# Top-k attention with a gated feed-forward block: the order of the left-over query tiles, the first loads, and where the weights' low words are converted

## The chip, the core and the metric

The kernel runs on one core of one Trainium2 chip. The metric is the time of one execution on the device, in microseconds (us). A core has a matrix engine (TensorE, PE in the profile), a vector engine (VectorE, DVE), an engine for pointwise functions (ScalarE, ACT), a general one (GpSimd, POOL) and one that here only issues transfers (SyncE, SP). Each works through its own list of instructions in order and waits where an operand or a buffer is not there yet. Matrix products land in PSUM, everything else is kept in SBUF, inputs and outputs lie in HBM and are moved by 16 DMA engines.

## The reference

Attention over 8 batches, 8 heads, 576 queries and keys of 64 elements, where each query keeps its 32 largest scores; then a feed-forward block over 4608 tokens.

```python
scores = scale * np.matmul(q, k.transpose(0, 1, 3, 2))            # (8, 8, 576, 576)
kth = np.partition(scores, -32, axis=-1)[..., -32:-31]
scores = np.where(scores >= kth, scores, -1e9)
attn = np.exp(scores - scores.max(-1, keepdims=True))
attn = attn / (attn.sum(-1, keepdims=True) + 1e-9)
x = np.matmul(attn, v)             # heads side by side: (4608, 512)
h = x @ w_in                       # w_in (512, 2048), given in 64-bit floats
g = h * np.clip(h + 3.0, 0.0, 6.0) / 6.0
out = g @ w_out                    # w_out (2048, 512), given in 64-bit floats
```

## The kernel before

**Tiles.** Two heads make a pair, two pairs a half of a batch. The 576 queries of a head are four tiles of 128 and a left-over of 64. A duo is one query tile of one half: four heads at 128 queries each, in two units of two rows of 576 scores. A left-over duo packs the 64 left-over queries of two heads into 128 partitions, so it has one row per unit instead of two, and half the work on VectorE. There are 80 duos: 64 full ones and 16 left-over ones.

**One duo.** `Duo.scores` (L201) multiplies on TensorE into the one five-bank PSUM tile `big` and copies to SBUF on ScalarE (L239, L242; L227, L228 for a left-over duo). `Duo.top` (L249) finds the 32 largest on VectorE: four rounds of MAX8 (L256), with MATCH_REPLACE8 (L260) between them. Then, late by a fixed number of slots: `shift` on GpSimd (L269, L272), `exp` on ScalarE (L279, L284), `inverse` on VectorE (L293), `weights` on GpSimd (L303, and a split into 16-bit halves, L312), `flip` as a DMA transpose (L318), `join` (L324, on ScalarE for the first unit, on GpSimd for the second), `values` on TensorE (L344) and `place` on ScalarE (L354).

**Slots.** The order of every engine's list is written out by a loop over duos and eight slots each (L576). Slot i of a duo issues one round of `top`; then come the delayed parts of earlier duos; in slot 1 the scores of the next duo. The delays are the tables at L538 to L551, in slots from the duo's start. For example, `weights` of the two units stand at 10 and 14, `join` at 15 and 19, `values` at 22 or 25; the last two duos have a shorter table.

**Feed-forward.** When both halves of a query tile have their values, a block of 128 tokens is queued (L480, L486): `feed_forward` (L358) cuts it into 16 pieces, eight of 8 products h (L371), eight of 2 products acc (L391). After every second h piece a gate follows on GpSimd (L385, L386), two pieces late. The loop issues pieces by a running sum (L609): one a slot while anything is queued, a little more when 24 or 48 pieces are queued, half of that in the slots of a left-over duo. What is left after the last slot is issued at the end (L612). Left-over tiles of an even batch and the odd one behind it share one block, in the tile `xr`.

**Weights.** They arrive as 64-bit floats and are turned into 32-bit ones in 32 chunks of 128 x 512 by `convert` (L96): a load into `st`, the high words' magnitude on ScalarE (L108) and clamped on GpSimd (L109), the low words on ScalarE (L111), two bit operations on VectorE (L117, L118), and an addition on GpSimd (L123). `convert_step` (L499) moves the stages on, once a slot from the first duo on. The temporaries `a` and `y` come from the pool `g` of eight buffers, which the feed-forward's `g` tiles use as well.

**The start.** L521 to L533: load the first pair (six transfers on SP's queue, k then q), start two weight chunks, load the second pair, transpose the first pair on TensorE into `big` and copy it out, three conversion steps and the scores of the first duo's two units among them.

**The order of duos** is the list built at L410 to L420, which the diff shows.

Of the kernel before, what the change touches and what calls it, by code (L numbers as in the profile page):

```python
# [8 lines left out]
AF = mybir.ActivationFunctionType  # L9
ALU = mybir.AluOpType  # L10
F32 = mybir.dt.float32
# [18 lines left out]
def kernel(  # L30
# [9 lines left out]
    nc = tc.nc  # L40
# [47 lines left out]
    def big():  # L88

        return ps_big.tile([P, 5 * 512], F32, tag="big", name="big")  # L90
# [5 lines left out]
    def convert(dst, src):  # L96

        st = kqpool.tile([P, 2 * WC], U32, tag="kq", name="st")
        nc.sync.dma_start(st[:], src)
        yield
        words = st[:].rearrange("p (n two) -> p n two", two=2)
        lo, hi = words[:, :, 0], words[:, :, 1]
        a = gpool.tile([P, WC], F32, tag="g", name="a")
        y = gpool.tile([P, WC], F32, tag="g", name="y")
        nc.scalar.activation(a[:], hi.bitcast(F32), AF.Abs)  # L108
        nc.gpsimd.tensor_scalar(a[:], a[:], HI_MOST, HI_LEAST, ALU.min, ALU.max)  # L109

        nc.scalar.activation(y[:], lo, AF.Copy, bias=2.0, scale=2.0**-51)  # L111
        yield

        au, yu = a[:].bitcast(U32), y[:].bitcast(U32)
        nc.vector.tensor_scalar(au, au, 3, None, ALU.logical_shift_left)  # L117
        nc.vector.scalar_tensor_tensor(  # L118
            out=yu, in0=hi, scalar=0x80000000, in1=yu,
            op0=ALU.bitwise_and, op1=ALU.bitwise_or,  # L120
        )
        yield
        nc.gpsimd.tensor_tensor(  # L123
            dst.bitcast(I32), a[:].bitcast(I32), y[:].bitcast(I32), ALU.add
        )

    def weight_chunks():
# [11 lines left out]
    class Pair:  # L139
# [3 lines left out]
            self.b, self.hp = b, hp  # L143
            self.vm, self.vr, self.kr = vms[hp], vrs[hp], krs[b % 2 * NHP + hp]

        def load(self):
            h0 = 2 * self.hp
            t = self.landed = kqpool.tile([P, 2 * J + 1, 2, D], F32, tag="kq", name="landed")
            for i, src in enumerate((k, q)):
                for hh in range(2):  # L150
                    nc.sync.dma_start(  # L151
                        t[:, i * J : (i + 1) * J, hh, :],
                        src[self.b, h0 + hh, 0:JP, :].rearrange("(p j) d -> p j d", j=J),
                    )
                nc.sync.dma_start(
                    t[i * R : (i + 1) * R, 2 * J, :, :],
                    src[self.b, h0 : h0 + 2, JP:S, :].rearrange("h s d -> s h d"),
                )
# [9 lines left out]
                    self.vr[hh * R : (hh + 1) * R, hh, :], v[self.b, h0 + hh, JP:S, :]  # L168
                )

        def transpose(self):
            kq = kqpool.tile([P, JP + S], F32, tag="kq", name="kq")
            self.kT, self.qT = kq[:, 0:JP], kq[:, JP : JP + S]
            ps = big()
            for j in range(2 * J + 1):
                rows = self.landed[:, j, :, :].rearrange("p h d -> p (h d)")
                nc.tensor.transpose(ps[:, j * P : (j + 1) * P], rows, ident[:])
            c0 = 2 * JP
            nc.scalar.copy(kq[:, 0:c0], ps[:, 0:c0])
            nc.scalar.copy(kq[:, c0 : c0 + R], ps[:, c0 + R : c0 + 2 * R])  # L180
            for hh in range(2):
                d = slice(hh * D, (hh + 1) * D)
                nc.scalar.copy(self.kr[d, hh, :], ps[d, c0 : c0 + R])

    class Duo:

# [14 lines left out]
        def scores(self, us=(0, 1)):  # L201

            if us[0] == 0:
                self.sc = scpool.tile([P, 2, 2 * (S + R)], F32, tag="sc", name="sc")
                self.den = mpool.tile([P, 2, 2], F32, tag="den", name="den")
            sc, nu = self.sc[:, us[0] : us[-1] + 1, :], len(us)
            ps = big()
            heads = [slice(0, D), slice(D, P)]
            qs = slice(self.qt * P, min(self.qt * P + P, S))
            banks = ps[:, 0 : 4 * 512].rearrange("p (n s) -> p n s", s=512)  # L210
            left = ps[:, 4 * 512 :]
            if self.rest:


                quarters = [
                    (i, hh, d, heads[u ^ hh])
                    for i, u in enumerate(us)
                    for hh, d in enumerate(heads)
                ]
                for i, hh, d, to in quarters:  # L220
                    pr = self.pairs[us[i]]
                    nc.tensor.matmul(banks[to, i, :], pr.qT[d, qs], pr.kT[d, :])
                for i, hh, d, to in quarters:
                    pr = self.pairs[us[i]]
                    nc.tensor.matmul(banks[to, 2 + i, 0:R], pr.qT[d, qs], pr.kr[d, hh, :])
                nc.gpsimd.memset(sc[:, :, S : S + R], 0.0)
                nc.scalar.copy(sc[:, :, 0:JP], banks[:, 0:nu, :])  # L227
                nc.scalar.copy(sc[:, :, JP:S], banks[:, 2 : 2 + nu, 0:R])  # L228
                return
            for i, u in enumerate(us):  # L230
                pr = self.pairs[u]
                nc.tensor.matmul(
                    left[:, i * P : (i + 1) * P], pr.qT[:, qs], pr.kr[:].rearrange("p h r -> p (h r)")
                )
            for i, u in enumerate(us):
                pr = self.pairs[u]
                for hh, d in enumerate(heads):
                    nc.tensor.matmul(banks[:, 2 * i + hh, :], pr.qT[d, qs], pr.kT[d, :])  # L238
            nc.scalar.copy(  # L239
                sc.rearrange("p u (h s) -> p (u h) s", h=2)[:, :, 0:JP], banks[:, 0 : 2 * nu, :]  # L240
            )
            nc.scalar.copy(  # L242
                sc[:, :, JP : JP + P], left[:, 0 : nu * P].rearrange("p (u r) -> p u r", r=P)
            )

        def row(self, u, t):
            return self.sc[:, u, t * S : (t + 1) * S]
# [162 lines left out]
    duos = []  # L410
    for b in range(B):
        halves = [pairs[b][0:2], pairs[b][2:4]]
        for qt in range(J):
            duos += [Duo(h, qt) for h in halves]


            if qt == (0 if b == B - 1 else J - 1) and not 2 < b < B - 1:
                duos += [Duo(h, J) for h in halves]
            elif 2 < b < B - 1 and qt % 2 == 0:
                duos.append(Duo(halves[qt // 2], J))  # L420
    assert J == NHP == 4
    per_batch = 2 * J + 2
    ND = len(duos)
# [68 lines left out]
    def land(count=1):  # L492

        for _ in range(min(count, len(chunks))):
            c = convert(*chunks.pop(0))
            next(c)
            landing.append(c)
# [21 lines left out]
        return pairs[b + 1][at - first] if b + 1 < B and 0 <= at - first < NHP else None  # L519

    first = pairs[0]  # L521
    first[0].load()
    land(2)
    first[1].load()
    first[0].transpose()
    convert_step()
    duos[0].scores((0,))
    convert_step()
    first[2].load()
    convert_step()  # L530
    first[1].transpose()
    duos[0].scores((1,))
    land()  # L533

# [41 lines left out]
    for m in range(ND + 3):  # L576
        u = duos[m] if m < ND else None
        for i in range(8):
# [2 lines left out]
            if m < 4:  # L581
                parts(8 * m + i, False)
            convert_step()
            if m == 0 and i == 0:
                first[3].load()
            if m == 0 and i in (1, 2):
                first[i + 1].transpose()
            if i == (4 if m == 0 else 1) and m + 1 < ND:
# [59 lines left out]
```

## Time and profile before

| What | us |
|---|---|
| Median of 9 runs | 1577.71 |
| Lowest, highest | 1576.16, 1578.34 |
| The profiled execution's own time | 1577.94 |
| Its span, first to last instruction | 1576.2 |
| VectorE busy | 1466.6 (93%) |
| TensorE busy | 1441.9 (91%) |
| GpSimd busy | 1144.9 (73%) |
| ScalarE busy | 1097.6 (70%) |

The profile is of one execution. "Busy" is the union of an engine's instructions; matmuls overlap one another and their ends are modelled, so a busy TensorE is not one at its peak. A line of the timeline gives the start in us, the duration, engine, source line, operation, output <- inputs, shapes and count, and in brackets the idle time before it with what ended it. A line of waits gives who waited for whom, with the total in us, the number of times and the longest. The mean granted TensorE clock was 0.962 of full speed.

### The profile page before, as it was taken

The page shows a single profiled execution, that of the slowest core. Times are in us where ns is not written, and L with a number is a line of the kernel's source. Part 1 is how long each engine was busy: PE and PEld are TensorE (multiplying, and loading weights), DVE is VectorE, ACT ScalarE, POOL GpSimd, SP SyncE. Part 2 cuts the span into 40 slices and gives each one's busy share as a digit, 9 for nine tenths or more (in the row PEclk, how much of TensorE's full clock was granted, in tenths as well). Part 3 has the DMA queues.
Part 4 walks back from the last instruction along what each step waited for, and adds up shares of the span by engine and source line. Part 5 has one row for each costly group of instructions (what it writes and reads, how often), then busy time and mean ns, then how long its engine had stood idle before and what let it go on. Part 6 is the DMA issues. An engine that isn't in the chain of part 4 may idle for free.

```text
span 1576.2 us, 28787 instructions
## 1 busy us (share of the span) xinstructions
PE 1441.9 (91%) x10272; PEld 1031.5 (65%) x10272; DVE 1466.6 (93%) x3105; ACT 1097.6 (70%) x1865; POOL 1144.9 (73%) x1264
## 2 busy tenths in 40 slices
PE   5355799879999999998999999998999999999899
PEld 3142666567767767676777777776777777776675
DVE  6999999999999999999999999999999999999700
ACT  6675776777877777777776786777776786777521
POOL 4868687777867777867687777867687777867841
PEclk9577899989999999999999999999999999999999
DMA  8652544444444543546254544445254444533410
GB/s 237 158 182 42 116 83 82 90 94 98 73 95 86 101 84 78 99 87 117 55 104 81 98 88 83 94 91 113 58 104 81 98 88 82 103 58 68 83 22 14
DMA packets 450319, 144.49 MB, mean 92 GB/s; under 512 B 433280, under 2 KB 441472, under 8 KB 450176
## 3 DMA queue, kind: packets, MB, share of 16 engines
q1 hardware_dynamic: 450176, 142.65, 43.8%
q8 instruction: 81, 1.33, 0.4%
q14 instruction: 62, 0.51, 0.1%
HBM read 45.09 MB, written 9.44 MB: 35 GB/s over the span
## 4 chain that ended last, share of the span: by engine, by line
DVE 78%; PE 12%; issue 4%; POOL 3%; ACT 2%; SPq 1%; DMA 0%; POOLq 0%
DVE m L256 40%; DVE wk L260 35%; PE acc L391 5%; PE h L371 5%; DVE y L118 1%; PE pv L344 1%; DVE a L117 1%; POOL e L312 1%; DVE den L293 1%; PE big L238 1%; POOL sc L303 1%; POOL eT L324 1%; ACT sc L284 1%; SPq L151 1%; POOL g L386 0%
## 5 line engine op out<-in xcount | busy, mean ns | idle before, releaser
L256 DVE MAX8 m<-wk 128x8 f32<-128x576 f32 x864 | 613.4, 747 | 2.2
L391 PE MATMUL acc<-w_out,g 128*128 128x512 f32 x1152 | 518.1, 601 | 18.1 <-POOL g L386 18.1
L371 PE MATMUL h<-xT,w_in 128*128 128x128 f32 x4096 | 482.8, 278 | 18.3 <-ACT xT L354 18.3
L371 PEld LDWEIGHTS h<-xT,w_in 128*128 128x128 f32 x4096 | 472.4, 194 | 40.6 <-ACT xT L354 18.3
L260 DVE MATCH_REPLACE8 wk<-m,wk 128x576 f32<-128x576 f32 x576 | 423.9, 743 | 0.0
L303 POOL TENSOR_SCALAR sc<-sc,den 128x576 f32<-128x576 f32 x288 | 214.0, 753 | 240.0 <-DVE den L293 221.3
L391 PEld LDWEIGHTS acc<-w_out,g 128*128 128x128 f32 x1152 | 213.5, 191 | 265.5 <-issue 238.4
L312 POOL COPY e<-sc 128x2304 uint16<-128x2304 uint16 (+1 forms) x192 | 320.4, 1679 | 10.2
L279 ACT ACTIVATE sc<-sc,m 128x576 f32<-128x576 f32 x288 | 209.9, 775 | 75.8 <-DVE m L256 75.4
L284 ACT ACTIVATE sc<-sc,shift 128x576 f32<-128x576 f32 x288 | 220.3, 768 | 52.4 <-POOL shift L272 50.5
L324 ACT COPY eT<-t 128x2304 uint16<-128x2304 uint16 (+1 forms) x82 | 216.0, 2634 | 44.1 <-DMA t<-e 39.5
L344 PE MATMUL pv<-eT,vm 128*64 128x128 f32 (+1 forms) x2560 | 164.0, 273 | 58.8 <-ACT eT L324 44.0
L260 DVE MATCH_REPLACE8 wk<-m,sc 128x576 f32<-128x576 f32 x288 | 211.9, 742 | 0.0
L344 PEld LDWEIGHTS pv<-eT,vm 128*64 128x64 f32 x2560 | 135.0, 141 | 110.4 <-ACT eT L324 48.2
L324 POOL COPY eT<-t 128x2304 uint16<-128x2304 uint16 (+1 forms) x78 | 203.9, 2614 | 4.2 <-DMA t<-e 4.0
L256 DVE MAX8 m<-sc 128x8 f32<-128x576 f32 x288 | 203.4, 743 | 1.7 <-ACT sc L242 1.7
L386 POOL TENSOR_TENSOR g<-g,hs 128x512 f32<-128x512 f32 x144 | 185.0, 1285 | 12.0
L379 ACT ACTIVATE g<-h,three 128x512 f32<-128x512 f32 x144 | 98.6, 684 | 134.3 <-PE h L371 123.6
L238 PE MATMUL big<-kq 64*128 64x512 f32 x512 | 136.1, 651 | 0.0
L239 ACT COPY sc<-big 128x2048 f32<-128x2048 f32 (+1 forms) x65 | 119.2, 1834 | 17.5 <-PE big L238 17.4
L385 POOL TENSOR_SCALAR g<-g 128x512 f32<-128x512 f32 x144 | 89.2, 620 | 51.8 <-ACT g L379 40.6
L381 ACT COPY hs<-h 128x512 f32<-128x512 f32 x144 | 83.6, 581 | 0.0
(47 smaller groups left out, 1026.2 us busy)
## 6 DMA issues: line engine op xcount, KB each, us to landing
landed<-in_k_dram SPq DMA_DIRECT2D x64, 128.0 KB, 3.1
landed<-in_q_dram SPq DMA_DIRECT2D x64, 128.0 KB, 3.0
st<-in_moe_w_in_dram SPq DMA_DIRECT2D x16, 512.0 KB, 5.1
vm<-in_v_dram SPq DMA_DIRECT2D x64, 128.0 KB, 2.4
st<-in_moe_w_out_dram SPq DMA_DIRECT2D x16, 512.0 KB, 6.2
out_dram<-o SPq DMA_DIRECT2D x32, 256.0 KB, 2.4
t<-e SPq DMA_TRANSPOSE x160, 4.6
landed<-in_k_dram SPq DMA_DIRECT2D x32, 32.0 KB, 2.9
```

The costliest lines, as they stand in the source:

```text
L238: nc.tensor.matmul(banks[:, 2 * i + hh, :], pr.qT[d, qs], pr.kT[d, :])
L256: nc.vector.max(self.m[u][:, t, 8 * r : 8 * r + 8], self.cur[t])
L260: nc.vector.match_replace(wk, self.m[u][:, t, 8 * r : 8 * r + 8], self.cur[t], LOWEST)
L279: nc.scalar.activation(row, row, AF.Prelu, bias=m[:, t, TOP_K - 1 : TOP_K], scale=-1.0, alpha=FLAT)
L284: nc.scalar.activation(row, row, AF.Exp, bias=self.less[u][:, t : t + 1], scale=-scale / FLAT, accum_out=self.den[:, u, t : t + 1],)
L303: nc.gpsimd.tensor_scalar(row, row, self.den[:, u, t : t + 1], 1.0, ALU.mult, ALU.mult)
L312: nc.gpsimd.tensor_copy(halves[:, :, to : to + c1 - c0], words)
L324: copy(eT[:, 0 : self.nb, :] .rearrange("p c q -> p (c q)") .bitcast(U16) .rearrange("p (x h) -> p h x", h=2), self.t16[u][:, 0 : 2 * self ...
L344: nc.tensor.matmul(pv[hh * D : (hh + 1) * D, u * w : (u + 1) * w], pr.vm[:, hh, c, :] if c < J else pr.vr[:, hh, :], rhs, start=(c == 0), ...
L371: nc.tensor.matmul(h[:, (f - f0) * P : (f - f0 + 1) * P], w_in[:, i, f * P : (f + 1) * P], xT[:, i, :], start=(i == 0), stop=(i == NHP - 1),)
L386: nc.gpsimd.tensor_tensor(g[:], g[:], hs[:], ALU.mult)
L391: nc.tensor.matmul(acc[:], gs[f // nf][:, f % nf * P : (f % nf + 1) * P], w_out[:, f, :], start=(f == 0), stop=(f == NFC - 1),)
```

## The change

Four things are changed.

1. The order of duos. Before, the left-over duos stood last in batches 0 to 2, one behind the first and one behind the third query tile in batches 3 to 6, and behind the first query tile in batch 7. Now they stand last in every even batch and first in every odd one, so that four of them follow one another at four places.
2. The start. VectorE zeroes a piece of `w_out`, and TensorE multiplies it twice into `big`, a result that nobody reads. The first pair's q is issued from ScalarE's queue, k from SP's. The loads of the second, third and fourth pair stand ahead of weight chunks that they stood behind. The first transposes go to three separate PSUM tiles, and what the first scores need is copied first; the remaining copies come behind the scores.
3. The first scores are copied out in three copies, the left-over keys first and then one head at a time.
4. In `convert`, the low words are converted into the destination (`dst`) instead of a temporary `y`, and the later steps work there in place.

```diff
@@ convert
-        y = gpool.tile([P, WC], F32, tag="g", name="y")
...
-        nc.scalar.activation(y[:], lo, AF.Copy, bias=2.0, scale=2.0**-51)
+        nc.scalar.activation(dst, lo, AF.Copy, bias=2.0, scale=2.0**-51)
...
-            out=yu, in0=hi, scalar=0x80000000, in1=yu,
+            out=dst.bitcast(U32), in0=hi, scalar=0x80000000, in1=dst.bitcast(U32),
...
-            dst.bitcast(I32), a[:].bitcast(I32), y[:].bitcast(I32), ALU.add
+            dst.bitcast(I32), a[:].bitcast(I32), dst.bitcast(I32), ALU.add
@@ Pair.load
-        def load(self):
+        def load(self, queue=None):
...
-            for i, src in enumerate((k, q)):
+            for i, (src, eng) in enumerate(((k, nc.sync), (q, queue or nc.sync))):
...
-                    nc.sync.dma_start(
+                    eng.dma_start(
@@ Pair.transpose
+            def turn(ps, tiles):
+                for i, j in enumerate(tiles):
+                    rows = self.landed[:, j, :, :].rearrange("p h d -> p (h d)")
+                    nc.tensor.transpose(ps[:, i * P : (i + 1) * P], rows, ident[:])
...
+            if first:
+                ps = [ps_w.tile([P, 512], F32, tag="w", name="kqp") for _ in range(3)]
+                turn(ps[0], range(J))
+                turn(ps[1], [J, 2 * J])
+                turn(ps[2], range(J + 1, 2 * J))
+                nc.scalar.copy(self.kT, ps[0][:])
+                nc.scalar.copy(kq[:, JP : JP + P], ps[1][:, 0:P])
+                copy_left(ps[1][:, P:])
+                self.later = [
+                    (kq[:, JP + P : c0], ps[2][:, 0 : JP - P]),
+                    (kq[:, c0 : c0 + R], ps[1][:, P + R : 2 * P]),
+                ]
+                return
@@ Duo.scores
+            if us == (0,):
+                (to, src), rest = copies
+                copies = [rest, (to[:, 0, :], src[:, 0, :]), (to[:, 1, :], src[:, 1, :])]
+            for copy in copies:
+                nc.scalar.copy(*copy)
@@ the order of duos
-        for qt in range(J):
+        for qt in [J, *range(J)] if b % 2 else range(J + 1):
             duos += [Duo(h, qt) for h in halves]
-            if qt == (0 if b == B - 1 else J - 1) and not 2 < b < B - 1:
-                duos += [Duo(h, J) for h in halves]
-            elif 2 < b < B - 1 and qt % 2 == 0:
-                duos.append(Duo(halves[qt // 2], J))
@@ the start
     first = pairs[0]
-    first[0].load()
-    land(2)
+    nc.vector.memset(w_out[:, 0, :], 0.0)
+    ps = big()
+    for _ in range(2):
+        nc.tensor.matmul(ps[:, 0:DM], w_out[:, 0, 0:P], w_out[:, 0, :])
+    first[0].load(nc.scalar)
     first[1].load()
-    first[0].transpose()
+    land()
+    first[2].load()
+    land()
+    first[0].transpose(first=True)
+    duos[0].scores((0,))
+    for copy in first[0].later:
+        nc.scalar.copy(*copy)
     convert_step()
-    duos[0].scores((0,))
+    first[3].load()
+    first[1].transpose()
     convert_step()
-    first[2].load()
-    convert_step()
-    first[1].transpose()
     duos[0].scores((1,))
     land()
@@ the loop over duos and slots
-            if m == 0 and i == 0:
-                first[3].load()
```

## The prediction

> **What bounds the kernel now.** I read the busy digits first, then VectorE's waits, then the two ends of the timeline. The page's second part, busy tenths in 40 slices of 39.4 us:
>
> ```profile
> PE   5355799879999999998999999998999999999899
> DVE  6999999999999999999999999999999999999700
> ```
>
> VectorE (DVE) is full from the second slice to the thirty-eighth, then stops while TensorE (PE) goes on. So there are three stretches: a head until DVE starts, a DVE stretch, a PE tail. What DVE waited for over the whole span (us in total, times, longest):
>
> ```profile
> DVE a L117 <- POOL a L109: 13.5, 2, 10.2
> DVE den L293 <- ACT den L289: 7.0, 2, 6.7
> DVE m L256 <- ACT sc L242: 1.7, 1, 1.7
> ```
>
> 10.2 us of the first row is the head, 6.7 of the second is the tail; between them DVE loses 3.6 us. Reading off the first MAX8 of each duo, duo 4 starts at 144.2 us and from there every full duo takes 19.40 us and every left-over duo 11.22 us, without one stall, to the last MAX8 at 1488.4 us. PE cannot shorten that stretch; it can only stall it. The head, from the timeline:
>
> ```profile
> 4.65 1.08 PE L177 MATMUL big<-ident,landed 128*128 128x128 f32 x4 [4.65 <-DMA landed<-in_k_dram]
> 6.88 1.30 PE L177 MATMUL big<-ident,landed 128*128 128x128 f32 x5 [1.15 <-DMA landed<-in_q_dram]
> 8.21 1.01 ACT L179 COPY kq<-big 128x1024 f32<-128x1024 f32 x1 [6.21 <-PE big L177]
> 10.45 2.08 PE L238 MATMUL big<-kq 64*128 64x512 f32 x4
> 12.58 1.01 ACT L239 COPY sc<-big 128x1024 f32<-128x1024 f32 x1 [1.68 <-PE big L238]
> 13.79 0.76 DVE L256 MAX8 m<-sc 128x8 f32<-128x576 f32 x1 [1.69 <-ACT sc L242]
> ```
>
> A chain of loads, transposes, copies, scores, copies. The tail, DVE's last MAX8 pair and PE after it:
>
> ```profile
> 1487.00 1.41 DVE L256 MAX8 m<-wk 128x8 f32<-128x576 f32 x2
> 1510.26 1.09 PE L344 MATMUL pv<-eT,vm 128*64 128x128 f32 x16
> ...
> 1512.60 3.70 PE L391 MATMUL acc<-w_out,g 128*128 128x512 f32 x8
> 1516.13 14.46 PE L371 MATMUL h<-xT,w_in 128*128 128x128 f32 x128
> 1530.42 13.90 PE L391 MATMUL acc<-w_out,g 128*128 128x512 f32 x32
> 1544.16 14.45 PE L371 MATMUL h<-xT,w_in 128*128 128x128 f32 x128
> 1558.45 13.90 PE L391 MATMUL acc<-w_out,g 128*128 128x512 f32 x32
> ```
>
> Behind the last value product come two pieces of an old feed-forward block and then two whole blocks. A block (16 pieces) starts 28.03 us after the one before it (1544.16 minus 1516.13): 1.75 us a piece. The tail is as long as the backlog.
>
> **What the Trainium skill says.** "DMA: Bandwidth & Descriptors", Issuing engines are not separate DMA queues: two issuing engines share the same 16 DMA engines and save only issue time. The trace has that time: six loads of one pair take SP from 0.72 to 4.77 us, about 0.68 each. "SBUF — State Buffer", Who interferes with whom: VectorE and GpSimd (POOL) share a port pair, and whichever comes second blocks for the other's whole instruction. The trace agrees: the conversion's second DVE step is 0.68 us at best and 1.75 at worst. "TensorE: Matmul & The Clock Gate", Part 1, gives about 3.4 us of work before full clock; here the clock is at full in the first 30 us anyway, and 0.50 at 40 to 60 us, so the warm-up should buy little.
>
> **The change, part by part.**
>
> *Order of the left-over duos.* No arithmetic is added or removed. The order matters through the feed-forward pacing: one piece a slot in full duos, half in left-over ones, none when the list is empty. Counting pieces slot by slot from the code: in the kernel before, 534 of 576 are placed by the end of the last duo's eight slots; with the new order, 542. In the old order the list runs dry in duos 12 to 14, 36 to 37 and 56 to 57, and the last left-over block is queued late in batch 7; in the new one it is dry only near duos 13 to 14. PE's program order agrees: behind the last value product stand 34 pieces before, 26 after. 8 x 1.753 = 14.0 us less tail.
> The pieces ahead of that product are 8 in both, but before, a gate (POOL 0.61 + 1.27, at 1488.14) stands ahead of the join that PE waits for at 1492.84; in the new order the pieces there are output products with no gate. That moves PE's end part 1.9 us earlier (0 to 2). I take 15.9.
>
> *Do the 8 pieces fit earlier?* From duo 10 to 79 PE would have 501 x 1.753 = 878 us of pieces, 56 x 4.93 (scores 2.60, values 2.33) for full duos, 14 x 2.5 for left-over ones and 28 transposes of about 1.0 us: 1217 us in 56 x 19.40 + 14 x 11.22 = 1243 us. Room of 26 us, about 2%. It fits, narrowly.
>
> *Four left-over duos in a row.* Next scores come up at slot 1 of the current duo and must be copied before it ends, 9.8 us later in a left-over duo against 17 in a full one. The worst margin before is at duo 30, behind two left-over duos (POOL, ACT and DVE timelines):
>
> ```profile
> 595.17 0.19 POOL L269 TENSOR_TENSOR shift<-m 128x1 f32<-128x1 f32 x1
> 595.72 0.78 ACT L284 ACTIVATE sc<-sc,shift 128x576 f32<-128x576 f32 x1 [3.02 <-POOL shift L272]
> 598.61 0.38 ACT L242 COPY sc<-big 128x256 f32<-128x256 f32 x1
> 599.64 1.40 DVE L256 MAX8 m<-sc 128x8 f32<-128x576 f32 x2
> ```
>
> Only 0.66 us remain. ACT's copy stands behind an exponential, and that behind POOL, which still works off full duos (two weight steps of 3.6, a join of 2.8). Two more left-over duos bring POOL 2 x 2.35 weights, 1.9 join, 0.9 shifts, 0.2 zeroing and 0 to 3.8 gates each: 7.7 to 11.5 us against 11.22. The backlog drains instead of growing, and copies for a left-over duo are 1.0 us shorter. Placed after DVE's steps, the third and fourth keep some 4 us. DVE cost: 0, bounds 0 to 2.5 us at each of four places.
>
> *First load on two queues, tiles ahead of weights.* q no longer waits behind k's three issues. Nine transposes at 0.26 from 4.65: the six needed end at 6.2. ACT: kT copy (about 0.58 by the 512-wide copy at L381) under the transposes, then 0.27 + 0.43, to 7.0. PE: 0.7 + 1.0 for the first head to 8.75, second at 9.8. ACT copies heads apart: 9.35 and 10.4. DVE starts at 9.4, and its second MAX8 waits 0.3. Gain 13.79 - 9.4 - 0.3 = 4.1 us (2 if q lands late on the shared engines, 5 at best).
> Against it, nine issues x 0.69 now stand ahead of the first weight chunk: issue at 6.9, landing 5.1 later at 12.0 (the page's median), then ACT 0.67 and POOL 0.61: 13.4, where DVE wants it at 12.6. Wait 0.8 (0 to 3). The second chunk is behind another pair: issued about 11.7, landed about 17, wanted near 18. The first chunk's DVE work sat in the idle head before (11.08 to 12.1); now all 32 stand behind the first MAX8: +1.4 (1.08 uncontended to 1.72, the mean of 54.9 us over 32 chunks).
>
> *Warm-up and zeroing.* DVE idles until 9.4. Two products at 0.43 a record x 2 records are 1.7 us, at half clock 3.4, from about 1.2: done by 4.65. Cost 0; without the cover, up to 1 us.
>
> *Low words converted in place.* Same instruction count; y no longer takes one of eight g buffers. ACT's longest early wait and what it did to DVE:
>
> ```profile
> 134.58 0.69 ACT L379 ACTIVATE g<-h,three 128x512 f32<-128x512 f32 x1 [9.08 <-POOL w_out L123]
> 137.12 1.48 DVE L117 TENSOR_SCALAR a<-a 128x512 uint32<-128x512 uint32 x1 [3.31 <-POOL a L109]
> ```
>
> Three chunks in flight plus four g of a block are 7 buffers instead of 10. I take the 3.3 us as gone (bounds 0 to 3.3). Unknown: the chunk's DVE steps take 54.9 us against 34.6 if never blocked by POOL; moved instants may change these 20 us either way, +-5.
>
> *Sum against the profiled span of 1576.2:* -15.9 - 4.1 + 0.8 + 1.4 - 3.3 = -21.1, so 1555.1. That execution took 1577.94, 1.74 more than its span, and the median is 1577.71: 1556.6 us, called 1556.5.
>
> **Rivals.**
> *Head gain eaten.* Later weight chunks and port blocking cost DVE what the earlier start gives: only the tail remains, 1577.7 - 15.9 = 1562. For it: 20 us of blocking there already; against: DVE's start itself moves on a plain chain.
> *PE or POOL just too late.* Small stalls, 2.5 us at each of four places: 1566.5. For it: the 0.66 us margin and the 2% room on PE; against: margins of 10 to 15 us in full duos.
> *The stretch of four becomes the bound.* If POOL's backlog grew through it, exponentials, score copies and then DVE would stop at each of four places. From 5.3 us each it eats the 21 us; at 7 us each the time is 1584, slower. For it, ACT's 3.02 us wait on POOL; against, 11.5 us at most of POOL work per 11.22 us.
> *Less blocking.* If ACT, no longer held, spreads the chunks, 7 of the 20 us go: 1549.
> *No effect in the tail*, if PE's pieces only slide within the same stream: excluded by the 34 and 26 counted.
>
> **How the numbers follow.** Likeliest case (1550 to 1561) 0.70; head gain eaten 0.12; small stalls 0.08; less blocking 0.06; four in a row as bound 0.04. I put the range at 1549 to 1566, leaving out most of the last case and the edges of two others. A difference under 0.2% (3.2 us) is about what cannot be told from no change. Faster 0.94, same 0.02, slower 0.04.
>
> **What would show it.** Right: first MAX8 near 9.4; duo 4 near 139; 19.40 and 11.22 us duos without stalls; last MAX8 near 1483; 26 pieces (45.6 us) behind the last value product; ACT's waits on the w_out addition gone. Wrong: MAX8 waiting on ACT's score copies in the third or fourth left-over duo or the full one behind; DVE waiting several us for the first chunks; PE idle in the middle, its pieces still in the tail.

## The result, and the profile after

The changed kernel takes 1570.55 us (median of 9 runs, 1568.43 to 1572.15), the kernel before 1577.95 in the runs beside it (29 runs, 1576.16 to 1579.8): a ratio of 0.9952, 95% interval 0.9943 to 0.9960. It is 7.4 us faster where 21 were forecast, and 1570.55 lies above the range. The profiled execution took 1570.55 and spans 1568.8.

The busy tenths of the changed kernel, each digit 39.2 us:

```profile
PE   5256799899999999999999999999999999999999
DVE  6999999999999998999999999999999999999910
```

VectorE (DVE) now has a dent at the sixteenth digit (588 to 628 us), and works one digit longer; TensorE (PE) is at nine tenths to the end. What VectorE waited for (total us, times, longest), in the changed kernel:

```profile
DVE den L318 <- ACT den L314: 16.9, 6, 6.0
DVE m L281 <- ACT sc L269: 9.8, 1, 9.8
```

Before, the first of these rows held 7.0 us in 2 waits, and 6.7 of it lay in the tail. Now 5.95 lies in the tail, and five others (2.32, 0.40, 4.68, 1.32 and 2.18 us, at 32, 593, 603, 1315 and 1484 us) lie where VectorE bounds the kernel. All are at one instruction, the reciprocal of the sum of exponentials (`inverse`, line 318). The second row is the head. The wait of 3.31 us for GpSimd (POOL) at 137 us is gone.

The head, from the timeline of the changed kernel (start, duration, engine, line, and in brackets the idle time before it and what ended it):

```profile
1.47 3.78 PE L548 MATMUL big<-w_out 128*128 128x512 f32 x4 [1.47 <-DVE w_out L545]
6.00 2.15 PE L180 MATMUL kqp<-ident,landed 128*128 128x128 f32 x9 [0.75 <-DMA landed<-in_k_dram]
...
8.99 1.38 PE L260 MATMUL big<-kq 64*128 64x512 f32 x4
10.42 1.24 ACT L269 COPY sc<-big 128x128 f32<-128x128 f32 x3 [2.22 <-PE big L260]
11.21 1.42 DVE L281 MAX8 m<-sc 128x8 f32<-128x576 f32 x2 [9.79 <-ACT sc L269]
```

In this execution the first MAX8 starts 2.6 us earlier than before. k lands later than it did (first transpose at 6.00 instead of 4.65), and the score copies begin at 10.42, with the last of the products (8.99 + 1.38) and not with the first. The execution is the latest of its kind: in the profiles of seven other runs below that have the same start, the first MAX8 lies between 9.75 and 10.42.

The tail of the changed kernel, PE's timeline from the last value product on:

```profile
1517.03 1.09 PE L369 MATMUL pv<-eT,vm 128*64 128x128 f32 x16
...
1519.36 3.84 PE L396 MATMUL h<-xT,w_in 128*128 128x128 f32 x32
1523.04 13.90 PE L416 MATMUL acc<-w_out,g 128*128 128x512 f32 x32
1536.78 14.45 PE L396 MATMUL h<-xT,w_in 128*128 128x128 f32 x128
1551.07 13.90 PE L416 MATMUL acc<-w_out,g 128*128 128x512 f32 x32
```

Counted as before, 2 + 8 + 8 + 8 = 26 pieces, the number of the prediction.

Taking the trace apart at three points, all in us (duo 4's first MAX8; VectorE's last MAX8; the end):

```
                          before   predicted   after
head, to duo 4             144.2       139.0   145.1
duo 4 to the last MAX8    1344.2      1344.2  1352.7
tail                        87.8        71.9    71.0
span                      1576.2      1555.1  1568.8
```

The tail came as forecast. 6.1 us are missing in the head, 8.5 in the middle. The 8.5 lie in three duos: duo 29 took 16.35 us instead of 11.23, duo 69 12.57, duo 79 21.75 (19.71 before). Every other duo from 4 on took 19.40 or 11.22 us, as forecast.

### The profile page after: what moved, and what is told of

Its sections match the earlier page's. It is cut to its first block, busy times and chain, and to the rows that moved or that the text cites. A ratio compares the mean times of both kernels' runs of the same rounds, so it can differ in the third digit from the quotient of the medians.

```text
span 1568.8 us, 28740 instructions
## 1 busy us (share of the span) xinstructions
PE 1448.6 (92%) x10276; PEld 1036.1 (66%) x10276; DVE 1470.8 (94%) x3106; ACT 1096.1 (70%) x1868; POOL 1144.5 (73%) x1264
## 4 chain that ended last, share of the span: by engine, by line
PE 57%; DVE 25%; POOL 6%; ACT 5%; issue 3%; DMA 2%; SPq 1%; POOLq 0%; ACTq 0%
PE h L396 22%; PE acc L416 21%; DVE m L281 12%; DVE wk L285 10%; PE pv L369 6%; PE big L260 5%; POOL e L337 2%; DMA t<-e 2%; POOL sc L328 1%; POOL eT L349 1%; DVE a L116 1%; PE big L254 1%; PE big L180 1%; DVE w_out L117 1%; ACT sc L309 1%
## 5 line engine op out<-in xcount | busy, mean ns | idle before, releaser
L349 ACT COPY eT<-t 128x2304 uint16<-128x2304 uint16 (+1 forms) x82 | 215.9, 2633 | 54.8 <-DMA t<-e 54.4
L349 POOL COPY eT<-t 128x2304 uint16<-128x2304 uint16 (+1 forms) x78 | 203.5, 2609 | 9.0 <-DMA t<-e 8.8
L269 ACT COPY sc<-big 128x256 f32<-128x256 f32 (+3 forms) x131 | 136.6, 1095 | 39.2 <-PE big L260 38.9
L260 PE MATMUL big<-kq 64*128 64x512 f32 x512 | 131.8, 634 | 0.0
```

The costliest lines, as they stand in the source:

```text
L349: copy(eT[:, 0 : self.nb, :] .rearrange("p c q -> p (c q)") .bitcast(U16) .rearrange("p (x h) -> p h x", h=2), self.t16[u][:, 0 : 2 * self ...
```

## Experiments: one part of the change at a time

**Order alone.** The kernel before with the new order of duos.

```diff
-        for qt in range(J):
+        for qt in [J, *range(J)] if b % 2 else range(J + 1):
             duos += [Duo(h, qt) for h in halves]
-            if qt == (0 if b == B - 1 else J - 1) and not 2 < b < B - 1:
-                duos += [Duo(h, J) for h in halves]
-            elif 2 < b < B - 1 and qt % 2 == 0:
-                duos.append(Duo(halves[qt // 2], J))
```

> The kernel before with the new order of duos alone. Theory of added terms (the shorter backlog is worth 15.9 us and nothing else moves): about 1562 us. Theory that VectorE is stopped by late transposes in the stretches of four left-over duos (4.7 + 1.3 us) and at the last duo but one (2.2 us): about 1570 us, with the same stops in the trace near duo 29.

1571.3 us, ratio 0.9954 (0.9942 to 0.9967): the whole measured gain. The tail is 72.5, 15.2 shorter; duo 4 starts at 144.0, but VectorE's last MAX8 is 8.9 later than before: duo 29 stops for 6.6 us, duo 51 for 0.5, duo 79 takes 21.76.

**Start alone.** The kernel before with the new loads, warm-up, first transposes and split copies.

> The kernel before with the new start and the split first copies alone. Prediction's terms: -4.1 + 0.8 + 1.4, about 1576 us. From the changed kernel's trace: first MAX8 at 11.2 instead of 13.8 us, and one more chunk behind it: 1575 to 1577 us.

1581.83 us, ratio 1.0025 (1.0014 to 1.0036): slower. The first MAX8 is at 10.13, 3.7 earlier than before; duo 1 starts only 0.9 earlier (44.2), and duo 4 3.6 later (147.8). The time is outside both expectations. The wait of 3.29 us for GpSimd's part of a chunk is still there in duo 3, and four of 0.5 to 2.4 us have joined it: three more for chunks, and one of 2.33 us at the reciprocal at 32 us.

**Conversion in place alone.** The kernel before with the new `convert`.

> The kernel before with the conversion in place alone. Prediction's term: -3.3, about 1574.6 us, with ScalarE's waits on the w_out addition gone. Rival: VectorE's conversion steps are blocked longer by GpSimd instead, and nothing is gained: 1577 to 1579 us.

1577.91 us, ratio 1.0001 (0.9993 to 1.0009): nothing. The wait at 137 us is gone as forecast, but the chunks' two DVE steps now take 58.2 us in all instead of 54.9: 3.3 us taken away, 3.3 given back.

So neither start nor conversion brought anything by itself, and the new order kept 6.4 of the 15.2 us by which it shortens the tail. The parts don't add up, either: by the spans, 6.4 less the 3.8 that the start costs alone leaves 2.6 us, and the changed kernel's span is 7.4 shorter.

## Experiments: what stops VectorE in the middle

At duo 29 the changed kernel's timeline reads as follows, VectorE, ScalarE (ACT), PE and SP's queue together:

```profile
586.73 3.70 PE L416 MATMUL acc<-w_out,g 128*128 128x512 f32 x8
590.47 0.60 ACT L426 ACTIVATE o<-acc 128x512 f32<-128x512 f32 x1 [3.25 <-PE acc L416]
591.10 0.36 SPq L428 DMA_DIRECT2D out_dram<-o  x1
591.56 8.15 SPq L343 DMA_TRANSPOSE t<-e  x3
597.37 2.80 ACT L349 COPY eT<-t 128x2304 uint16<-128x2304 uint16 x1 [3.12 <-DMA t<-e]
603.03 0.20 ACT L314 ACTIVATE den<-den 128x1 f32<-128x1 f32 x1
603.27 0.16 DVE L318 RECIPROCAL den<-den 128x1 f32<-128x1 f32 x1 [4.68 <-ACT den L314]
604.03 0.27 ACT L250 COPY sc<-big 128x128 f32<-128x128 f32 x1
605.66 0.74 DVE L281 MAX8 m<-sc 128x8 f32<-128x576 f32 x1
```

Read upwards: the reciprocal waits for the exponentials; these stand on ACT behind a copy of the transposed weights (L349), and that waited for a transposing DMA. The DMA stood on SP's queue behind an output transfer (591.10), which waited for ACT's `o`, which waited 3.25 us for PE's last output product. So two theories: SP's queue is held by the output transfer, or PE is late and everything that ACT does in order behind PE's results is late with it. PE's lateness can be measured: the start of a duo's first score product against VectorE's first MAX8 of the duo before it, worked out from both timelines (us):

```
duo          12    16    20    24    28    32    40    60    68
before      5.1  -0.8  -1.2  -2.2  -1.3   3.1   3.8   3.7   0.2
after       5.1   3.2   6.7   6.2   7.9  -0.6   1.6   5.1   6.2
```

It is over 6 us at duos 28 and 68, just ahead of the stops.

**Output transfers on ScalarE's queue.** Line 428, `nc.sync` to `nc.scalar`.

> The changed kernel with its output transfers issued from ScalarE's queue instead of SP's. Theory that an output transfer, waiting for a late TensorE, holds SP's queue and with it the DMA transposes, and that VectorE's stops set the end: the stops at duos 29 and 69 go, 1562 to 1565 us. Theory that TensorE itself is the bound: the stops shrink but the end stays, 1568 to 1571 us.

1579.35 us, ratio 1.0010 (1.0002 to 1.0018), 8.8 slower than the changed kernel and outside both expectations. The transposing DMA is no longer held, but the stops are more, at duos 27 to 29, 48, 49 and 69: ACT waits for PE directly (between 570 and 620 us 3.2 us at `o`, and 2.7 in three waits at `g`). So freeing SP's queue does not take the stops away. The run alone does not clear the queue, because it also makes PE later (its lag is 12.3 us at duo 28 and 8.9 at 68); the next runs vary PE's lateness itself.

**Less work for PE.** The changed kernel, and the kernel before, with 2 of the 16 output products left out in the first 30 of 36 blocks; their rows of the output lack that part of the sum.

```diff
+        n_acc = NFC - 2 if count[0] <= 30 else NFC
...
+            if f < n_acc:
+                nc.tensor.matmul(
...
+                    stop=(f == n_acc - 1),
```

> The changed kernel with the last two of 16 output products left out in the first 30 of 36 feed-forward blocks (so these rows are incomplete): 30 x 1.75 = 52 us less for TensorE, none of it in the tail. Theory that a late TensorE holds ScalarE, and ScalarE VectorE's reciprocals: no stops at duos 29 and 69, the tail as it is, 1560 to 1565 us. Theory that the stops come from the transposes or from ScalarE's and GpSimd's own work in the stretches of four: stops as they are, 1567 to 1571 us. Theory that the end follows TensorE's total: far below, 1520 to 1545 us.

1564.42 us, ratio 0.9916 (0.9902 to 0.9929): 6.1 below the changed kernel. PE's lag is -0.5 at duo 28 and -0.5 at 68, and the stops at duos 29 and 69 are gone; that at 79, where nothing is left out, stays (21.74).

> The kernel before with the same products left out (the same rows are incomplete). VectorE has no stops there that a late TensorE could cause, and the tail is untrimmed, so 1576 to 1579 us. If the end follows TensorE's total: 1525 to 1550 us.

1577.81 us, ratio 1.0002 (0.9994 to 1.0010). The kernel before gains nothing from 52 us less on PE. So PE's lateness stops VectorE in the new order, and did not in the old. Across the runs the stop grows with the lag: lags of 7.0, 7.9 and 9.0 us at duo 28 (weights first, below; the changed kernel; the order alone) go with 4.2, 5.1 and 6.6 us lost in duo 29, and lags of 3.3, 4.6 and 6.2 at duo 68 (the order alone, weights first, the changed kernel) with 0, 0 and 1.3 in duo 69.

**Three pieces held back.** The changed kernel, where a piece is placed only when more than three wait.

```diff
-            due += ((left > 0) + ...
+            due += ((left > 3) + ...
```

> The changed kernel with the pacing holding back its last three pieces until more are queued, so that TensorE has work when a new block waits for its operand. Theory that TensorE's lag is fed by the 0.51 us waits at each block's start and makes the stops: no waits, a smaller lag at duos 28 and 68, stops gone, 1562 to 1567 us, with up to three pieces (5 us) more in the tail. Rival, the lag has other sources: 1570 to 1576 us.

1567.17 us, ratio 0.9934 (0.9921 to 0.9946). No work is taken away, the lag at duos 28 and 68 is -2.4, and no stop is left, also at 79 (19.71). In the profiled execution, which took 1568.87, VectorE ends 8.4 us earlier and the tail is 6.7 longer (three more pieces in it): the reserve that removes the lag is paid for in the tail. What PE waits for between 250 and 1470 us, first in the changed kernel, then with three pieces held back (total us, times, longest):

```profile
PE h L396 <- ACT xT L379: 10.1, 20, 0.5
PE h L396 <- ACT xr L379: 6.6, 4, 4.3
```

```profile
PE big L180 <- ACT sc L250: 7.7, 3, 2.6
PE big L244 <- ACT kr L185: 3.4, 2, 1.7
```

Total idle time is nearly the same (19.6 and 18.3 us). But in the changed kernel it is lost on blocks whose input ACT has only just copied, 0.5 us twenty times; with a reserve PE waits for the next score slot, which is what being early looks like.

**The reciprocal one slot later.** The changed kernel; the weights on GpSimd move with it, the slots of the DMA transposes (`flip`) and PE's order stay.

```diff
-    shift0=3, exp0=4, inverse0=9, weights0=10, ... inverse1=13, weights1=14,
+    shift0=3, exp0=4, inverse0=10, weights0=11, ... inverse1=14, weights1=15,
```

> The changed kernel, with each reciprocal on VectorE and the weights behind it one slot (some 2.4 us) later in the schedule; TensorE's order is the same. If the reciprocal is the door by which a late chain on TensorE and ScalarE stops VectorE: the waits of 4.68 at duo 29, 1.32 at duo 69 and 2.18 at duo 79 shrink by about 2.4 each, to 2.3, 0 and 0, and the time falls by 4 to 6 us, to 1565 to 1567. If VectorE is stopped at the reciprocal only because that stands first, and the next score copies are as late: MAX8 waits in its place, and the time stays within 1 us of 1570.6. If GpSimd or the transposing DMA then becomes late: slower.

1596.25 us, ratio 1.0121 (1.0108 to 1.0135): 26 us slower, the third case of the expectation. VectorE now waits for `den` 13 times, 38.0 us in all, and after the first MAX8 there are 12 more at which VectorE waits for score copies (7.8 us), as the second case had it. A reason shows in ACT's waits for the transposing DMA, first in the changed kernel, then here:

```profile
ACT eT L349 <- DMA t<-e: 54.4, 28, 6.0
```

```profile
ACT eT L349 <- DMA t<-e: 176.8, 56, 7.5
```

Reciprocal, GpSimd's weights, transposing DMA, ACT's copy of the transposed weights, the next exponentials behind that copy, and the next reciprocal form a ring. Giving the reciprocal time takes it from the DMA, and ACT passes the delay back. The ring is read from these waits; its links weren't tried singly, and neither was a move of the reciprocal with the transposes moved along. This move did not help; taking PE's lateness away did.

**Held back and given back.** As with three held back, and one extra piece in 16 slots from duo 72 on, so that 26 pieces stand behind the last value product again.

```diff
+            due += ((m >= 72) / 16 + (left > (3 if m < 76 else 0)) + ...
```

> The changed kernel, with three feed-forward pieces held back as before, and given back: one extra piece in 16 slots over the last eight duos. Counted from the code, 26 pieces stand behind the last value product, as in the changed kernel, where holding three back without giving them back had 29. If a late TensorE is what stops VectorE in the middle: no stop at duos 29 and 69, last MAX8 near 1489 to 1491 us, tail near 71 to 72, time near 1561 to 1563 us. If what was won by holding back was bought with the tail and the two can't be had together: a stop comes back at duos 76 to 79 and the time stays at 1566 us or above.

1565.38 us, ratio 0.9924 (0.9912 to 0.9937). No stop at 29 and 69; last MAX8 at 1491.0, tail 72.4; but duo 79 has its stop again (2.15 us). Between the two expectations, 2.4 above the first one's upper end: duo 79's stop belongs to the pieces that come early there. In the changed kernel it is a gate: GpSimd's two gate steps at 1475.86 to 1477.83 stand ahead of its weights and the shift, ACT's exponential waits 5.01 us for that shift, and the reciprocal 2.18 for the exponential. In the run that holds three back to the end, the shift stands ahead of that gate (1472.99 and 1473.58), and there is no stop.

## Experiments: where the head's gain goes

**Weights first.** The changed kernel with loads, chunks and conversion steps in the order of the kernel before; two queues, warm-up and split copies stay.

```diff
     first[0].load(nc.scalar)
-    first[1].load()
-    land()
-    first[2].load()
-    land()
+    land(2)
+    first[1].load()
     first[0].transpose(first=True)
+    convert_step()
     duos[0].scores((0,))
...
-    first[3].load()
+    first[2].load()
+    convert_step()
     first[1].transpose()
-    convert_step()
...
+            if m == 0 and i == 0:
+                first[3].load()
```

> The changed kernel with the two-queue first load, the warm-up and the split copies, but the other pairs and the weight chunks loaded and converted in the order of the kernel before. Theory that the loads moved ahead of the weights cost what the earlier start gives: duo 4 starts 3 us earlier than in the changed kernel, 1566 to 1568 us. Rival, the time goes to port blocking whatever the order of the loads: 1570 to 1572 us.

1566.98 us, ratio 0.9937 (0.9924 to 0.9949): 3.6 below the changed kernel by the medians, but two of its five executions took 1569.7 and 1570.4. In the profiled one, of 1566.98, 1.4 is the head (duo 4 at 143.7; the first chunk's two VectorE steps lie ahead of the first MAX8 again); the rest is the stop at duo 69, gone, and that at 29, 4.2 instead of 5.1.

**The old start with the pieces held and given back; and weights first with the same.**

> The kernel before with two edits: the new order of left-over duos, and the pieces held back and given back. Its start and its conversion of weights are those of the kernel before. If start and conversion bring nothing: duo 4 near 144.0 us, no stop in the middle, last MAX8 near 1489, tail 71, time near 1561 to 1562 us, the same as with the new start within 1.5 us, and 16 below the kernel before, which is the tail's gain that the prediction counted. If the new start brings its 4 us once nothing else stands in the way: 4 us slower than the version with it.

1564.33 us, ratio 0.9917 (0.9903 to 0.9930), duo 4 at 143.8. The kernel with the old start and the old conversion is 1.05 below the one with the new: the two bring nothing here either. The time is 2.3 above the first expectation's upper end; duo 79 has its stop here too (21.74).

> The changed kernel with the loads, weight chunks and first conversion steps in the order of the kernel before (two queues, warm-up and split copies stay), and the pieces held back and given back. If the two gains add: duo 4 near 143.7, no stop in the middle, tail near 71, time near 1560 to 1561 us, some 10 below the changed kernel. If they are one gain seen twice (both only make TensorE less late): no more than 1 us below the version that only holds pieces back and gives them back.

1563.69 us, ratio 0.9913 (0.9899 to 0.9926), duo 4 at 143.8. 1.7 below the version with the new order of loads, between the two expectations: once PE isn't late, only the head's 1.0 us and some tail are left of its 3.6.

**GpSimd's phase**, that is, the instants at which its steps fall against VectorE's. In duo 3 of the changed kernel VectorE and GpSimd meet like this:

```profile
139.78 2.17 POOL L337 COPY e<-sc 128x2304 uint16<-128x2304 uint16 x1
139.91 2.58 DVE L117 SCALAR_TENSOR_TENSOR w_out<-st,w_out 128x512 uint32<-128x512 uint32 x1
```

A step that takes 0.68 us undisturbed started 0.13 behind a GpSimd copy and ended 0.5 behind that copy's end. The chunk steps of duo 3 take 17.4 us (16 steps), before 12.0 (14 steps). In the run with all reciprocals one slot later they took 13.6, and duo 4 started at 140.9. So the same move for duos 2 and 3 alone, on the version that holds and gives back:

```diff
+    later = dict(usual, inverse0=10, weights0=11, inverse1=14, weights1=15)
...
+        elif m < 4:
+            when = later
```

> The changed kernel with pieces held back and given back, and with reciprocals and weights of duos 2 and 3 alone one slot later. If the gain of start and conversion in place is lost to GpSimd's phase in duo 3: VectorE's conversion steps there fall from 17.5 to about 13.5 us, duo 4 starts near 141 instead of 144.8, and the time falls from 1565.4 to 1561 or 1562. If only the later GpSimd schedule of all duos gave that phase: duo 4 stays at 144 to 145 and the time at 1565.

1562.2 us, ratio 0.9900 (0.9887 to 0.9914), 3.2 below. Duo 4 at 141.8; the copy is past, and that step, now at 140.77, takes 1.09 us.

> The kernel before with the new order and the pieces held back and given back, and reciprocals and weights of duos 2 and 3 one slot later. Start and conversion are the old ones, so ScalarE's wait for a g buffer and VectorE's wait of 3.3 us at 137 us stay, and there is little phase to win: duo 4 near 143 to 144, time 1563.5 to 1564.5, 2 to 3 above the same edit with the new start. If the move of the reciprocals is the gain and the start none: duo 4 near 140 to 141 and the same time as with the new start.

1565.2 us, ratio 0.9920 (0.9906 to 0.9934): with the old start and conversion the same move gains nothing (duo 4 at 144.2). The wait of 3.3 us, which was expected to stay, is gone here without the conversion in place, and all chunk steps together go up from 54.9 to 58.6 us: again what the wait lost came back as blocking. So the move isn't a gain by itself, and start and conversion together do hold 3 us, which this phase lets out.

**The reciprocal at 32 us.** The first place in the head where VectorE is held, once MAX8 has begun, is again the reciprocal. ACT and VectorE in the changed kernel:

```profile
22.48 0.66 ACT L107 ACTIVATE a<-st 128x512 f32<-128x512 f32 x1 [2.37 <-DMA st<-in_moe_w_in_dram]
27.29 1.01 ACT L203 COPY kq<-big 128x1024 f32<-128x1024 f32 x1 [0.98 <-PE big L180]
28.76 1.44 ACT L304 ACTIVATE sc<-sc,m 128x576 f32<-128x576 f32 x2
31.74 0.20 ACT L314 ACTIVATE den<-den 128x2 f32<-128x2 f32 x1
31.98 0.17 DVE L318 RECIPROCAL den<-den 128x2 f32<-128x2 f32 x1 [2.32 <-ACT den L314]
```

The exponentials stand on ACT behind a pair's copies (27.29 to 28.73), which wait for PE's transposes and not for MAX8. Those transposes wait for ACT's copies of the pair before (23.60 to 25.02), and these stand on ACT behind the high words of a weight chunk, for whose landing ACT waited 2.37 us. So the tile loads that were put ahead of the weights have a part in it: ACT takes its fourth chunk at 22.48, and in the kernel before it took it at 22.01, although MAX8 began later there. In eight executions with the changed kernel's start, ACT waits 2.1 to 2.5 us for that chunk and VectorE 2.3 at the reciprocal; in the two with weights first, ACT has no such wait and the reciprocal 0.6 and 0.8. The first MAX8 of the eight lies between 9.75 and 11.21, and duo 1 between 43.9 and 44.7 all the same. Duo 1 comes no earlier with weights first (44.5 and 44.7): there a chunk's conversion stands ahead of the first score copies on ACT, and the first MAX8 is at 11.59. The last run puts the steps of duos 0 and 1 one slot later too:

```diff
-        shift0=3, exp0=3, inverse0=4, weights0=4, flip0=5, join0=8,
-        shift1=7, exp1=7, inverse1=8, weights1=8, flip1=9, join1=12, values=12, place=13,
+        shift0=3, exp0=3, inverse0=5, weights0=5, flip0=6, join0=9,
+        shift1=7, exp1=7, inverse1=9, weights1=9, flip1=10, join1=13, values=13, place=14,
```

> As the first of these three, with reciprocals, weights, flips, joins and values of duos 0 and 1 one slot later too. If the start's gain is swallowed at the reciprocal at 32 us, whose own chain on ScalarE doesn't move: that wait of 2.3 us goes, duo 1 starts near 41.8 instead of 44, and duo 4 near 139: time 1559 to 1560. If the next score copies or GpSimd's steps are no earlier either: VectorE waits or is blocked there instead, and nothing is won over the first of the three.

1561.68 us, ratio 0.9897 (0.9884 to 0.9911): not told apart from 1562.2. The wait of 2.3 us is gone, and duo 1 starts at 43.5, not at 41.8: VectorE waits for chunks instead (0.3 to 1.0 us, four times), and its chunk steps of duo 0 take 13.4 us instead of 12.2. This run and the first of the three beat both kernels: they are 9 and 8 us below the changed one.

## Why the prediction was wrong, step by step

The span came out 13.7 us longer than forecast. Two steps failed: that the pieces fit earlier (6.5 us), and that the head's gains reach duo 4 (6.1 us: 2.4 of them ahead of duo 1, the rest in duo 3). A stop in duo 79, which was not reckoned, adds 2.0, and the tail gained 0.9 more than forecast.

*What bounds the kernel* held: VectorE to its last MAX8, then PE's backlog. The kernel before is indifferent to 52 us of PE work, as that reading requires.

*Order of the left-over duos* held: 26 pieces, and 51.8 us from the last value product to the end where it was 65.9, 14.1 less (14.0 forecast). The way from VectorE's last MAX8 to that product became 2.6 us shorter (1.9 forecast).

*Do the 8 pieces fit earlier?* is the first step that failed, worth 6.5 us at duos 29 and 69. Its sum was not far off: 26 us of room in 1243 were reckoned, and PE was idle for 19.6 in the 1220 us from 250 on. The conclusion "it fits, narrowly" was wrong because an average room was taken for room at each place. In a full duo PE and VectorE need nearly the same time (by the prediction's own figures 8 x 1.753 + 4.93 = 19.0 us, or 20.0 with a pair's transposes, against 19.40), so a lag of 6 us isn't worked off: it grew from 3.2 at duo 16 to 7.9 at duo 28. In the old order the list ran dry at three places, and PE caught up there: its lag fell to -13.5, -4.8 and -4.8 at duos 15, 38 and 58. The prediction named these gaps and counted them only as pieces not done. The new order fills these gaps; that is the tail's gain, and also the loss of the places where lateness ended. That is read from the lags; no run fills the gaps in the old order. The run that leaves products out and the one that holds three pieces back both take the lag away, by different means, and both lose the two stops. Which part of the second's effect is the reserve at a block's start, and which the three pieces' own 5.3 us, isn't separated.

*Four left-over duos in a row* looked at the right place, duos 28 to 31, but at the wrong instruction. Only the margin of the score copies ahead of MAX8 was worked out. No MAX8 waited there: the copies end at 604.3, and MAX8 takes them at 605.66. But that is so because the reciprocal had stopped VectorE before; 4.7 us earlier, at 601.0, the copies would have been 3.3 us late, not the "some 4 us" early that were reckoned. The reciprocal stands in VectorE's own order among the MAX8 steps and waits for ACT's exponentials, which stand ahead of the copies; no margin was worked out for it, and none for a late PE. The bounds of 0 to 2.5 us at each of four places were exceeded at one (5.1) and not used at two. GpSimd's backlog, which the step reckoned, was not the cause: the cause was PE, through ACT's order.

*First load on two queues, tiles ahead of weights.* The forecast was -4.1, +0.8 and +1.4. The first MAX8 came 2.6 us earlier in the changed kernel's profile and 3.4 to 4.0 in the seven others with this start, so 9.4 was nearly met, but in part by luck: two errors work against each other. k's first transpose begins at 5.45 to 6.24 us in all eleven profiles with two queues, against 4.40 to 4.77 in the six with one. Here the statement of the Trainium skill that the prediction quoted ("DMA: Bandwidth & Descriptors", Issuing engines are not separate DMA queues) applied to a step that had taken k's landing as fixed. What SP issues behind k begins no earlier than before (3.03 us instead of 2.81), so it is q's transfers that now run beside k's. Against this, the warm-up made the products faster (below). The copies "heads apart" split only the copying: ACT's first one waited for all four products. The wait for the first two chunks was nothing in the changed kernel's profile and 0.6 to 1.9 us in the seven others. The step that failed is that this gain was carried on to duo 4, with nothing reckoned behind the second chunk: a later chunk holds ACT at 22 us, and VectorE waits 2.32 us at the reciprocal. In the profile duo 0 took 33.01 us instead of 31.26, so 0.9 of the 2.6 reached duo 1. The reciprocal is not the only bar: with its wait gone, the last run's duo 1 still started at 43.5. Starting a bound engine earlier gains nothing where its next stop doesn't come earlier too.

*Low words converted in place.* The 3.3 us wait went, as forecast, and came back as blocking, within the "+-5" that was set aside for it; the sum took the gain at full value and the blocking at zero. This is shown by the run with this edit alone, and from the other side by the two runs that move the reciprocals of duos 2 and 3. With the new start's extra chunk behind the first MAX8 (+1.4 forecast), duo 3 became 1.9 us longer where 1.9 shorter was expected.

*Warm-up and zeroing* cost nothing, as forecast; it was done by 5.25 us, ahead of the transposes at 6.00. That it "should buy little", since the clock is at full anyway, was a misreading. The granted clock reads 1.00 in both kernels over the first 10 us, and yet the first four score records take 2.08 us in all six profiles without the warm-up and 1.13 in ten of the eleven with it; nine transposes take 1.17 instead of 2.38 where the warm-up has worked by then (with three pieces held back, for one). The changed kernel's own profile is the eleventh: its transposes still took 2.15 and its score records 1.38. Another run whose transposes began at 6.00 as well (products left out) took 1.17 and 1.13 and had its first MAX8 at 10.19 instead of 11.21. No run takes the warm-up out by itself.

*Duo 79's stop*, 2.0 us, stood nowhere in the prediction. In all runs with the new order but one (three pieces held back to the end) it comes with the earlier pieces; by the traces of the changed kernel and of that one run it is a gate's place on GpSimd. This was read and not tried by itself.

*The rivals.* "Head gain eaten" (1562) and "PE or POOL just too late" (1566.5) both came true, and were priced as alternatives. The forecast without the head's gain, 5.2 higher, and with 8.5 of stops is 1570. Since one has its place in the first 144 us and the other behind it, nothing let them exclude each other, and the range should have reached their sum.

## To carry to other kernels

Where a secondary engine is to take work earlier, compare its time with the bound engine's per step and not over the stretch: if they are about equal, gaps in its work are where it catches up, and filling them keeps every lag. List every instruction on the bound engine that waits for another one, small ones first, with a margin for each; here a reciprocal of 0.16 us, for which no margin had been worked out, stopped VectorE first. A gain at the start counts only as far as the next such instruction also comes earlier.

## What the runs showed of the hardware that was not expected

- With q issued from a second queue, k's first transpose began at 5.45 to 6.24 us (eleven profiles) instead of 4.40 to 4.77 (six), although k's own issues began at 0.72 every time.
- With two products on a zeroed tile ahead of them (begun at 1.47, 3.4 to 3.8 us long) the first four score records took 1.13 us instead of 2.08 in ten profiles of eleven. The granted clock of the profile, 1.00 with and without them, doesn't show this.
- VectorE's 32 chunk conversions took between 54.7 and 58.8 us with the same instructions on the same data; one step of 0.68 us took 2.58 beside a GpSimd copy. This agrees with "SBUF — State Buffer", Who interferes with whom, in the Trainium skill, and prices it: 4 us, as much as each part of the start was meant to bring. Two different edits (the conversion in place alone; the reciprocals of two duos later, with the old start) each removed the 3.3 us wait in duo 3 and got 3.5 us of longer chunk steps there in return.
- One slot (2.4 us) of shift in the reciprocals of 0.16 us and the weights behind them cost 26 us over the changed kernel, with waits around a ring of three engines and a DMA.
